# Seven half-width block products in place of eight in the output projection of an attention and SwiGLU kernel

## The chip, the cores and the metric

The kernel runs on one core of one Trainium2 chip. The metric is device time in microseconds (us) of one execution. Most executions agree within 0.3%. Three kinds of figures appear. Total times and ratios come from timed rounds. Stage lengths come from a profiled execution. The span in a profile is 1.6 to 2.1 us shorter than the time of the same execution.

## The reference

Sliding-window attention (batch 8, 8 heads, 576 positions, head size 64, window 32 to each side), then a SwiGLU block on the 4608 tokens: 512 features in, 1536 hidden, 512 out.

```python
attn = softmax(where(|i - j| <= 32, q @ k.T / 8, -1e9))
x    = (attn @ v) as [4608, 512]
out  = (silu(x @ w_gate) * (x @ w_val)) @ w_out
```

## The kernel before

The tokens are worked off in nine chunks of 512, counted from 0. In each chunk twelve units produce the gate and value products (TensorE), silu (ScalarE) and their product `hT` (VectorE). Then a stage follows that multiplies `hT` by `w_out`. This stage is interleaved with the attention of the next chunk: four tiles m to m+3, each with scores (`s_mm`), exponential on ScalarE (`s_exp`), mask on VectorE (`s_mask`), value matmuls (`a_mm`), normalization on VectorE (`a_norm`), and a transposing DMA into the next chunk's `xT` (`x_dma`). In the timelines below each engine starts its instructions in the order of the program. Matmuls add up their results in tiles of the accumulation memory PSUM; I call such a tile of 128 x 512 fp32 numbers a bank. I call "the stage" the time from its first score matmul to the first gate matmul of the next chunk. The code is shortened, with short lines joined.

```python
htpool = ...tile_pool(name="ht", bufs=2)
ps_a = ...tile_pool(name="ps_a", bufs=3, PSUM)   # scores, values, u_ps
ps_o = ...tile_pool(name="ps_o", bufs=2, PSUM)   # gate products, output products
# ... cut ...
def ffn2_part(j, sub, lo, hi):
    if lo == 0:
        obs[sub] = ps_o.tile([128, 512], FP32, tag="o", name="ob")
    for fk in range(lo, hi):
        nc.tensor.matmul(out=obs[sub], lhsT=hts[j][:, fk, 128*sub:128*sub+128],
                         rhs=wo16[:, fk, :], start=(fk == 0), stop=(fk == FKS - 1))
# ... cut ...
def ffn2(j, m):
    s_group((m, m + 1)); s_mask(m); s_mask(m + 1)
    ffn2_part(j, 0, 0, 6); ffn2_part(j, 0, 6, FKS)
    s_group((m + 2, m + 3))
    a_group((m,)); x_dma(m)
    s_mask(m + 2); s_mask(m + 3)
    ffn2_part(j, 1, 0, 8); ffn2_out(j, 0)
    a_group((m + 1, m + 2, m + 3))
    for i in (1, 2, 3): x_dma(m + i)
    ffn2_part(j, 1, 8, FKS); ffn2_out(j, 1)
    for sub in (2, 3):
        ffn2_part(j, sub, 0, FKS); ffn2_out(j, sub)
# ... cut ...
for j in range(1, NCH):
    a = ffn1_two(j)                      # units 0 and 1
    for u in range(2, FKS):
        ffn1_unit(j, u)
        if u == 2 and j + 1 < B: fetch(j + 1, a)      # GpSimd issues v and token loads
        if u >= 8 and j + 1 < B: shift(j + 1, 2 * (u - 8) + 1)   # two v copies on VectorE
    if j + 1 < NCH: ffn2(j, 4 * j + 4)
```

Of the kernel before, what the change touches and what calls it, by code (L numbers as in the profile page):

```python
# [7 lines left out]
FP32 = mybir.dt.float32  # L8
FP16 = mybir.dt.float16
# [3 lines left out]
ALU = mybir.AluOpType  # L13
# [3 lines left out]
def general_path(tc, keep, ident, weights, q, k, v, out):  # L17
# [6 lines left out]
    FKS = wg16.shape[2] // 128  # L24
    GS = d_model // 128
    BIG = 1.0e9
    with ExitStack() as st:
# [78 lines left out]
        with tc.For_i(0, B * S, 128) as r:  # L106
            xn = sb.tile([128, d_model], FP32, name="g_xn")
            nc.sync.dma_start(out=xn, in_=xd[bass.ds(r, 128), :])
            xT = sb.tile([128, GS, 128], FP16, name="g_xT")
            for g in range(GS):  # L110
                px = ps.tile([128, 128], FP32, name="g_px")
# [3 lines left out]
            for f in range(FKS):  # L115
                gv = ps.tile([128, 2, 128], FP32, name="g_gv")
                for i, w in enumerate((wg16, wv16)):
                    for g in range(GS):
                        nc.tensor.matmul(out=gv[:, i, :], lhsT=w[:, g, 128 * f:128 * f + 128],
                                         rhs=xT[:, g, :], start=(g == 0), stop=(g == GS - 1))  # L120
                sl = sb.tile([128, 128], FP16, name="g_sl")
# [12 lines left out]
def kernel(  # L134
# [10 lines left out]
    nc = tc.nc  # L145

    B, H, S, D = q.shape
    d_model, d_ff = moe_w_gate.shape
# [5 lines left out]
    NCH = n_tokens // 512  # L154
    FKS = d_ff // 128
    GS = d_model // 128
    SLABS = (0, 2, 4, 6, 9, 12)
    LONG = 2
    TP = 9
# [5 lines left out]
    fast = ctx.enter_context(ExitStack())  # L165
    const = fast.enter_context(tc.tile_pool(name="const", bufs=1))
# [5 lines left out]
    xtpool = fast.enter_context(tc.tile_pool(name="xt", bufs=3))  # L172
    htpool = fast.enter_context(tc.tile_pool(name="ht", bufs=2))
    spool = fast.enter_context(tc.tile_pool(name="sp", bufs=4))
    opool = fast.enter_context(tc.tile_pool(name="op", bufs=4))
    ps_a = fast.enter_context(tc.tile_pool(name="ps_a", bufs=3, space=bass.MemoryType.PSUM))
    ps_o = fast.enter_context(tc.tile_pool(name="ps_o", bufs=2, space=bass.MemoryType.PSUM))
    fast.enter_context(tc.manual_schedule())

    ident = keep.tile([128, 128], FP16)  # L180
    wg16 = keep.tile([128, GS, d_ff], FP16)
    wv16 = keep.tile([128, GS, d_ff], FP16)
    wo16 = keep.tile([128, FKS, d_model], FP16)
# [11 lines left out]
    kT = [const.tile([128, HP, S + 64], FP16, name=f"kT{i}") for i in range(2)]  # L195
    qT = [const.tile([128, HP, S], FP16, name=f"qT{i}") for i in range(2)]
    v16 = [const.tile([128, NT, H, 66], FP16, name=f"v16{i}") for i in range(2)]

    def after(dma, inst):
        tc.add_manual_dep(  # L200
            dma.ins, inst.ins.name,
            mybir.DependencyInfo(mybir.DependencyClass.Sync, mybir.DependencyReason.DATA),
            reason="load order")

    def cp_act(o, i):
        return nc.scalar.activation(out=o, in_=i, func=AF.Copy, bias=0.0, scale=1.0)  # L206

    def cp_dve(o, i):
        nc.vector.tensor_copy(out=o, in_=i)  # L209
# [13 lines left out]
    def load_long16(src, b, x):  # L223
        return long_dma((nc.gpsimd, nc.gpsimd), st16.tile([128, 2, TP * D], FP16, tag="st16", name="st16"),
                        src, b, x)
# [36 lines left out]
    def load_v(b, blocks, gate=None):  # L262
        vb = v[b].rearrange("h s d -> s h d")
        for m in blocks:
            lo, hi = max(0, 128 * m - 32), min(S, 128 * m + 96)
            p0 = lo - (128 * m - 32)
            d = nc.gpsimd.dma_start(out=v16[b % 2][p0:p0 + hi - lo, 2 * m, :, 0:D], in_=vb[lo:hi])  # L267
            if gate is not None:
                after(d, gate)

    def shift_v(b, t0, t1, lo, hi):
        vb = v16[b % 2]
        if lo:
            lo(vb[0:64, t0:t1:2], vb[64:128, t0 - 1:t1 - 1:2])
        if hi:
            hi(vb[64:128, t0:t1:2], vb[0:64, t0 + 1:t1 + 1:2])

    def load_w(s, which):
        c0, c1 = 128 * SLABS[s], 128 * SLABS[s + 1]
        for i in which:  # L280
            w, w16 = ((moe_w_gate, wg16), (moe_w_val, wv16))[i]
            nc.gpsimd.dma_start(
                out=w16[:, :, c0:c1],
                in_=w.rearrange("(g p) c -> p g c", p=128)[:, :, c0:c1])
# [6 lines left out]
    def load_tok(src, b, gate=None):  # L291
        st = stpool.tile([128, 5, H, D], FP16, tag="st", name="tok")
        sb = src[b].rearrange("h s d -> s h d")
        for m in range(5):
            n = min(128, S - 128 * m)
            d = nc.gpsimd.dma_start(out=st[0:n, m], in_=sb[128 * m:128 * m + n])  # L296
            if gate is not None:
                after(d, gate)
        return st
# [58 lines left out]
    def s_mask(m):  # L358
        p = pts[m].rearrange("p g i h q -> p (g i h q)")
        nc.vector.tensor_tensor(out=p, in0=p, in1=mask.rearrange("p a q -> p (a q)"),  # L360
                                op=ALU.mult)
# [32 lines left out]
    def x_out(m):  # L394
        j, i4 = divmod(m, 4)
        if j not in xts:
            xts[j] = xtpool.tile([128, 4, GS, 128], FP16, tag="xt", name="xT")
        return xts[j][:, i4]
# [15 lines left out]
    def x_dma(m):  # L414
        x16 = x16s.pop(m).rearrange("p a h d -> p (a h d)")
        nc.sync.dma_start_transpose(out=x_out(m), in_=x16)

    hts = {}
# [40 lines left out]
    def ffn1_two(j):  # L459
        for lo in (0, 256):  # L460
            for fk in range(2):
                ffn1_mm(j, fk, lo, 256, lo)
        return [ffn1_out(j, fk, 0, 512) for fk in range(2)][0]
# [13 lines left out]
    def ffn2_out(j, sub, parts=1):  # L477
# [5 lines left out]
            nc.sync.dma_start(out=out[r0:r0 + 128, c:c + w], in_=osb[:, c:c + w])  # L483
        return a

    def ffn2_last(j, sub):
        r0 = 512 * j + 128 * sub
        for c, w in ((0, 256), (256, 128), (384, 128)):
            ob = ps_o.tile([128, 512], FP32, tag="o", name="ob")
            for fk in range(FKS):  # L490
                nc.tensor.matmul(  # L491
                    out=ob[:, 0:w],
                    lhsT=hts[j][:, fk, 128 * sub:128 * sub + 128],
                    rhs=wo16[:, fk, c:c + w],
                    start=(fk == 0), stop=(fk == FKS - 1))
            osb = opool.tile([128, d_model], FP32, tag="osb", name="osb")
            cp_dve(osb[:, 0:w], ob[:, 0:w])
            nc.scalar.dma_start(out=out[r0:r0 + 128, c:c + w], in_=osb[:, 0:w])
# [60 lines left out]
    kq = []  # L559
    for s in range(len(SLABS) - 1):  # L560
        if s == 2:
            shift_v(0, 5, 6, cp_pool, cp_pool)
            shift_v(0, 7, 8, cp_pool, cp_pool)
        if s == len(SLABS) - 2:
            kq.append((load_long16(k, 1, 0), kT[1], 0, 32))
# [57 lines left out]
    for u in range(2):  # L623
        ffn1_unit(0, u, 256, 256)
    nc.vector.tensor_copy(
        out=mask, in_=band.unsqueeze(1).to_broadcast([128, 4 * HP, 64]))
# [20 lines left out]
    def fetch(b, gate):  # L647
        if len(toks[b]) == 1:
            toks[b].append(load_tok(q, b, gate))
        load_v(b, range(5), gate)  # L650
        if b + 1 < B:
            toks[b + 1] = [load_tok(k, b + 1), load_tok(q, b + 1)]
        kt, qt = toks.pop(b)
        turn_tok(kt, kT[b % 2], 32)
        turn_tok(qt, qT[b % 2], 0)

    def s_group(ms):
        for m in ms:
            s_mm(m)
            s_exp(m)  # L660

    def a_group(ms):
        for m in ms:
            a_mm(m)
            a_norm(m)
# [31 lines left out]
    def ffn2(j, m):  # L697
        s_group((m, m + 1))
        s_mask(m)
        s_mask(m + 1)  # L700
        ffn2_part(j, 0, 0, 6)
        ffn2_part(j, 0, 6, FKS)
        s_group((m + 2, m + 3))
        a_group((m,))
        x_dma(m)
        s_mask(m + 2)
        s_mask(m + 3)
        ffn2_part(j, 1, 0, 8)
        ffn2_out(j, 0)
        a_group((m + 1, m + 2, m + 3))  # L710
        for i in (1, 2, 3):
            x_dma(m + i)
        ffn2_part(j, 1, 8, FKS)
        ffn2_out(j, 1, 2 if j == NCH - 2 else 1)
        for sub in (2, 3):
            ffn2_part(j, sub, 0, 6)
            ffn2_part(j, sub, 6, FKS)
            ffn2_out(j, sub, 2 if j == NCH - 2 and sub in (2, 3) else 1)

    ffn2_first(4)  # L720
    for j in range(1, NCH):
        a = ffn1_two(j)
        for u in range(2, FKS):
            ffn1_unit(j, u)
            if u == 2 and j + 1 < B:
                fetch(j + 1, a)
            if u >= 8 and j + 1 < B:
                shift(j + 1, 2 * (u - 8) + 1)
        if j + 1 < NCH:
            ffn2(j, 4 * j + 4)  # L730
        else:
            good = check_range()
            for sub in range(3):
                ffn2_part(j, sub, 0, 6)
                ffn2_part(j, sub, 6, FKS)
                if sub == 1:
                    count_good(good)
                ffn2_out(j, sub, 2)
            ffn2_last(j, 3)
# [35 lines left out]
```

## Time and profile before

| | before |
|---|---|
| median time, 3 runs | 329.0 us |
| TensorE, VectorE, ScalarE busy | 98%, 49%, 46% |
| chain that ended last, TensorE's part | 94% |
| stage of each of the chunks 1 to 7 | 13.0 us |

In a timeline row the first number is the start in us from the span's begin, the second the length. `x12` means twelve instructions merged. A bracket gives the idle time of that engine before the row and what ended it; idle times up to 0.15 us get no bracket. The pages and rows of the kernel before stand in the prediction.

### The profile page before, as it was taken

To read this page: it belongs to the slowest core of one execution; us is meant where nothing else is said; L and a number is where in the kernel's file an instruction comes from. 1 tells how busy PE (TensorE), PEld (TensorE's weight loads), DVE (VectorE), ACT (ScalarE), POOL (GpSimd) and SP (SyncE) were. 2 spreads that over 40 slices of the span, in tenths; PEclk is the share of its full clock that TensorE was granted. 3 is DMA by queue.
4 is the path that set the end of the run, shared out by engine and by line. 5 is a ranking of instruction groups with operands and counts; after the bars stand their busy time and mean duration, and the time that the engine had idled before them with its cause. 6 is when DMAs were issued, how large, how long until landed. Compare 5 with 4: busy or idle time off the path is not lost.

```text
span 326.8 us, 6917 instructions
## 1 busy us (share of the span) xinstructions
PE 319.5 (98%) x2769; PEld 169.6 (52%) x2769; DVE 160.1 (49%) x319; ACT 151.3 (46%) x215; POOL 104.6 (32%) x136
## 2 busy tenths in 40 slices
PE   7999999999999999999999999999999999999994
PEld 5564546445554555455644564456445644564443
DVE  5754874457145734474347524762367143714421
ACT  4843675337443724372536453544355434643320
POOL 8964605964096007800680048203100000000000
PEclk9999999999999999999999999999999999999999
DMA  9999999999999959994999489988913400150012
GB/s 154 184 199 203 199 143 191 137 156 154 204 132 149 83 134 165 151 109 104 182 138 135 99 146 131 155 112 166 149 19 64 131 0 2 50 146 2 1 54 82
DMA packets 155190, 40.14 MB, mean 123 GB/s; under 512 B 140816, under 2 KB 151184, under 8 KB 155152
## 3 DMA queue, kind: packets, MB, share of 16 engines
q0 software_dynamic: 102640, 18.59, 76.5%
q1 hardware_dynamic: 51936, 20.49, 32.8%
q10 hardware_dynamic: 576, 0.56, 0.6%
q8 instruction: 23, 0.38, 0.5%
q14 instruction: 15, 0.12, 0.1%
HBM read 37.75 MB, written 9.44 MB: 144 GB/s over the span
## 4 chain that ended last, share of the span: by engine, by line
PE 94%; POOL 3%; DMA 2%; issue 0%; DVE 0%; POOLq 0%; DVEq 0%
PE g_ps L424 29%; PE u_ps L424 29%; PE ob L471 29%; PE o_ps L377 3%; PE s_ps L343 3%; DMA wg<-in_moe_w_gate_dram 2%; POOL v L267 1%; POOL st L213 1%; PE ob L491 1%; PE t_ps L248 1%; PE xt_ps L404 0%; DVE osb L209 0%; POOL iota L525 0%; PE cnt L515 0%; DVEq L209 0%
## 5 line engine op out<-in xcount | busy, mean ns | idle before, releaser
L451 DVE TENSOR_TENSOR hT<-ssb,u_ps 128x512 f16<-128x512 f16 (+1 forms) x110 | 74.5, 678 | 130.2 <-PE u_ps L424 78.1
L424 PE MATMUL g_ps<-xT,wg 128*128 128x512 f16 (+1 forms) x504 | 114.0, 349 | 0.2 <-DMA wg<-in_moe_w_gate_dram 0.2
L424 PE MATMUL u_ps<-xT,wv 128*128 128x512 f16 (+1 forms) x504 | 114.0, 349 | 0.0
L449 ACT ACTIVATE ssb<-g_ps 128x512 f16<-128x512 f32 (+1 forms) x110 | 64.7, 589 | 100.9 <-PE g_ps L424 100.5
L471 PE MATMUL ob<-wo,hT 128*128 128x512 f16 x420 | 95.5, 380 | 0.0
L424 PEld LDWEIGHTS <-wv 128*128 128x128 f16 x504 | 49.3, 98 | 44.2
L424 PEld LDWEIGHTS <-wg 128*128 128x128 f16 x504 | 48.9, 98 | 43.4 <-DMA wg<-in_moe_w_gate_dram 0.3
L267 POOL DMA_DIRECT2D v<-in_v_dram x40 | 33.7, 863 | 91.1 <-ACT ssb L449 90.0
L471 PEld LDWEIGHTS <-hT 128*128 128x128 f16 x420 | 39.0, 98 | 44.3
L206 ACT ACTIVATE osb<-ob 128x512 f32<-128x512 f32 x35 | 21.0, 599 | 51.9 <-PE ob L471 51.9
L353 ACT ACTIVATE p_t<-s_ps 128x1024 f16<-128x1024 f32 x36 | 34.9, 1022 | 4.7 <-PE s_ps L343 4.6
L296 POOL DMA_DIRECT2D tok<-in_k_dram x30 | 25.3, 879 | 14.2 <-ACT osb L206 12.6
L296 POOL DMA_DIRECT2D tok<-in_q_dram x30 | 25.5, 854 | 11.7 <-DMA v<-in_v_dram 4.8
L360 DVE TENSOR_TENSOR p_t<-p_t,mask 128x1024 f16<-128x1024 f16 x32 | 21.4, 688 | 9.3 <-ACT p_t L353 9.2
L389 DVE TENSOR_TENSOR x<-o_ps,rall 128x512 f16<-128x512 f32 x36 | 24.9, 691 | 1.2
L209 DVE COPY v<-v 64x528 f16<-64x528 f16 x60 | 18.5, 308 | 2.3 <-DMA v<-in_v_dram 0.4
L343 PEld LDWEIGHTS <-kT 64*128 64x128 f16 x576 | 9.7, 95 | 8.1 <-issue 7.2
L377 PEld LDWEIGHTS <-p_t 128*64 128x64 f16 x576 | 10.9, 110 | 4.9 <-DVE p_t L360 3.0
L377 PE MATMUL o_ps<-v,p_t 128*64 128x66 f16 x576 | 13.1, 196 | 0.2 <-ACT p_t L353 0.2
L343 PE MATMUL s_ps<-qT,kT 64*128 64x64 f16 x576 | 12.1, 191 | 0.1
L449 ACT ACT_TABLE_LOAD x8 | 10.3, 1283 | 0.1
L353 ACT ACT_TABLE_LOAD x8 | 10.3, 1283 | 0.1
(59 smaller groups left out, 87.6 us busy)
## 6 DMA issues: line engine op xcount, KB each, us to landing
out_dram<-osb SPq DMA_DIRECT2D x29, 256.0 KB, 2.3
v<-in_v_dram POOLq DMA_DIRECT2D x24, 128.0 KB, 6.4
tok<-in_k_dram POOLq DMA_DIRECT2D x24, 128.0 KB, 8.7
tok<-in_q_dram POOLq DMA_DIRECT2D x24, 128.0 KB, 9.8
v<-in_v_dram POOLq DMA_DIRECT2D x16, 96.0 KB, 6.3
wo<-in_moe_w_out_dram POOLq DMA_DIRECT2D x3, 512.0 KB, 9.2
out_dram<-osb SPq DMA_DIRECT2D x12, 128.0 KB, 1.8
st<-in_q_dram POOLq DMA_DIRECT2D x8, 144.0 KB, 6.5
```

The costliest lines, as they stand in the source:

```text
L206: return nc.scalar.activation(out=o, in_=i, func=AF.Copy, bias=0.0, scale=1.0)
L267: d = nc.gpsimd.dma_start(out=v16[b % 2][p0:p0 + hi - lo, 2 * m, :, 0:D], in_=vb[lo:hi])
L296: d = nc.gpsimd.dma_start(out=st[0:n, m], in_=sb[128 * m:128 * m + n])
L343: nc.tensor.matmul(out=sts[m][:, g, i, hp, :], lhsT=kT[b % 2][64 * g:64 * g + 64, hp, 64 * t:64 * t + 128], rhs=qT[b % 2][64 * g:64 * g + ...
L353: nc.scalar.activation(out=p.rearrange("p g i h q -> p (g i h q)"), in_=s.rearrange("p g i h q -> p (g i h q)"), func=AF.Exp, bias=0.0, sc ...
L360: nc.vector.tensor_tensor(out=p, in0=p, in1=mask.rearrange("p a q -> p (a q)"), op=ALU.mult)
L377: nc.tensor.matmul(out=o[64 * i:64 * i + 64, h // 4, 66 * (h % 4):66 * (h % 4) + 66], lhsT=p[:, g, i, hp, :], rhs=v16[b % 2][:, t, h, :], ...
L389: nc.vector.tensor_tensor(out=x16, in0=ov[:, :, :, 0:D], in1=r.unsqueeze(3).to_broadcast([128, 2, 4, D]), op=ALU.mult)
L424: nc.tensor.matmul(out=ps[:, at:at + n], lhsT=w[:, g, 128 * fk:128 * fk + 128], rhs=xts[j][:, lo // 128:(lo + n) // 128, g, :], start=(g = ...
L449: a = nc.scalar.activation(out=ssb[:, 0:n], in_=ps[0][:, 0:n], func=AF.Silu, bias=0.0, scale=1.0)
L451: nc.vector.tensor_tensor(out=hts[j][:, fk, lo:lo + n], in0=ssb[:, 0:n], in1=ps[1][:, 0:n], op=ALU.mult)
L471: nc.tensor.matmul(out=obs[sub], lhsT=hts[j][:, fk, 128 * sub:128 * sub + 128], rhs=wo16[:, fk, :], start=(fk == 0), stop=(fk == FKS - 1))
```

## The change

A 2x2x2 split of the product (tokens, hidden, output columns each in two halves) is computed with seven block products of a Strassen type and not eight. The aim is to take an eighth of TensorE's work out of this product in chunks 1 to 7. It is paid for with sums of fp16 blocks on VectorE (`sum_a` on `hT` each chunk, `sum_b` on `w_out` once), three fp32 snapshots of partial sums on ScalarE and three output additions on VectorE. A snapshot is a copy of a partial sum out of its bank, taken before the bank takes in the next product. The core of the diff, shortened and with lines joined:

```diff
+    def sum_a(j, i, lo, hi):       # s1 = a21+a22, s2 = s1-a11, s3 = a11-a21, s4 = a12-s2
+        ...
+    def prod(ps, lhs, rhs, first):
+        for kk in range(KH):                      # KH = 6
+            for i in range(2):
+                nc.tensor.matmul(out=ps[:, 256*i:256*i+256], lhsT=lhs[:, kk, 128*i:128*i+128],
+                                 rhs=rhs[:, kk], start=(first and kk == 0 and i == 0), ...)
+    def ffn2_seven(j, m):
+        s_group((m, m + 1)); s_mask(m); s_mask(m + 1)
+        sum_a(j, 3, KH - 2, KH)
+        x = bank(); prod(x, a11, b11, True); p1 = keep_act(x)
+        z = bank(); prod(z, s1, t1, True)
+        s_group((m + 2, m + 3)); a_group((m,)); x_dma(m)
+        s_mask(m + 2); s_mask(m + 3)
+        prod(x, s2, t2, False); u2 = keep_act(x)
+        a_group((m + 1, m + 2, m + 3)); x_dma(m + 1) ... x_dma(m + 3)
+        prod(x, s3, t3, False); u3 = keep_act(x)
+        y = ps_a.tile(...); prod(y, a12, b21, True)
+        put_sum(j, z, u3, 1, 1); put_sum(j, y, p1, 0, 0)
+        prod(x, a22, t4, False); o = out_tile(); cp_act(o, x); put(j, o, 1, 0)
+        prod(z, s4, b22, False); put_sum(j, z, u2, 0, 1)
     ...
             ffn1_unit(j, u)
+            if j == 1 and 2 <= u < 6: sum_b(u - 2)
+            if j + 1 < NCH:
+                if u in (4, 6):     sum_a(j, 2, ...)           # 768 elements
+                if u in (7, 9, 11): sum_a(j, 0, ...); sum_a(j, 1, ...)   # 512 each
+                if u == 10:         sum_a(j, 3, 0, KH - 2)     # 1024
             if u >= 8 and j + 1 < B: shift(j + 1, 2 * (u - 8) + 1)
-            ffn2(j, 4 * j + 4)
+            ffn2_seven(j, 4 * j + 4)
```

More of the change, by code (lines that the diff above doesn't have):

```diff
@@ L156 @@
     GS = d_model // 128
+    KH = FKS // 2
+    CH = d_model // 2
     SLABS = (0, 2, 4, 6, 9, 12)
@@ L174 @@
     spool = fast.enter_context(tc.tile_pool(name="sp", bufs=4))
+    snap = fast.enter_context(tc.tile_pool(name="sn", bufs=3))
     opool = fast.enter_context(tc.tile_pool(name="op", bufs=4))
@@ L197 @@
     v16 = [const.tile([128, NT, H, 66], FP16, name=f"v16{i}") for i in range(2)]
+    sumA = [const.tile([128, KH, 256], FP16, name=f"sa{i}") for i in range(4)]
+    sumB = [const.tile([128, KH, CH], FP16, name=f"sb{i}") for i in range(4)]
     def after(dma, inst):
@@ L484, in ffn2_out, with comb, sum_b @@
         return a
+    def comb(o, a, b, op):
+        nc.vector.tensor_tensor(out=o, in0=a, in1=b, op=op)
+    def sum_b(i):
+        b11, b12 = wo16[:, 0:KH, 0:CH], wo16[:, 0:KH, CH:]
+        b21, b22 = wo16[:, KH:, 0:CH], wo16[:, KH:, CH:]
+        t1, t2, t3, t4 = sumB
+        o, a, b = ((t1, b12, b11), (t2, b22, t1), (t3, b22, b12), (t4, b21, t2))[i]
+        comb(o, a, b, ALU.subtract)
+    def sum_a(j, i, lo, hi):
+        h = hts[j]
+        a11, a12 = h[:, lo:hi, 0:256], h[:, KH + lo:KH + hi, 0:256]
+        a21, a22 = h[:, lo:hi, 256:512], h[:, KH + lo:KH + hi, 256:512]
+        s1, s2, s3, s4 = [t[:, lo:hi] for t in sumA]
+        o, a, b, op = ((s1, a21, a22, ALU.add), (s2, s1, a11, ALU.subtract),
+                       (s3, a11, a21, ALU.subtract), (s4, a12, s2, ALU.subtract))[i]
+        comb(o, a, b, op)
@@ new lines, in prod, with bank, keep_act @@
+    def prod(ps, lhs, rhs, first):
+        for kk in range(KH):
+            for i in range(2):
+                nc.tensor.matmul(out=ps[:, CH * i:CH * i + CH],
+                                 lhsT=lhs[:, kk, 128 * i:128 * i + 128], rhs=rhs[:, kk],
+                                 start=(first and kk == 0 and i == 0),
+                                 stop=(kk == KH - 1 and i == 1), skip_group_check=True)
+    def bank():
+        return ps_o.tile([128, 512], FP32, tag="o", name="ob")
+    def keep_act(ps):
+        t = snap.tile([128, 512], FP32, tag="sn", name="sn")
+        cp_act(t, ps)
+        return t
@@ new lines, in out_tile, with put, put_sum @@
+    def out_tile():
+        return opool.tile([128, d_model], FP32, tag="osb", name="osb")
+    def put(j, o, row, col):
+        r0 = 512 * j + 256 * row
+        nc.sync.dma_start(
+            out=out[r0:r0 + 256, CH * col:CH * col + CH].rearrange("(i p) c -> p i c", p=128),
+            in_=o.rearrange("p (i c) -> p i c", i=2))
+    def put_sum(j, ps, sn, row, col):
+        o = out_tile()
+        comb(o, ps, sn, ALU.add)
+        put(j, o, row, col)
+    def ffn2_seven(j, m):
+        h = hts[j]
+        a11, a12, a22 = h[:, 0:KH, 0:256], h[:, KH:, 0:256], h[:, KH:, 256:512]
+        b11, b21, b22 = wo16[:, 0:KH, 0:CH], wo16[:, KH:, 0:CH], wo16[:, KH:, CH:]
+        s1, s2, s3, s4 = sumA
+        t1, t2, t3, t4 = sumB
+        s_group((m, m + 1))
+        s_mask(m)
+        s_mask(m + 1)
+        sum_a(j, 3, KH - 2, KH)
+        x = bank()
+        prod(x, a11, b11, True)
+        p1 = keep_act(x)
+        z = bank()
+        prod(z, s1, t1, True)
+        s_group((m + 2, m + 3))
+        a_group((m,))
+        x_dma(m)
+        s_mask(m + 2)
+        s_mask(m + 3)
+        prod(x, s2, t2, False)
+        u2 = keep_act(x)
+        a_group((m + 1, m + 2, m + 3))
+        for i in (1, 2, 3):
+            x_dma(m + i)
+        prod(x, s3, t3, False)
+        u3 = keep_act(x)
+        y = ps_a.tile([128, 512], FP32, tag="a", name="y_ps")
+        prod(y, a12, b21, True)
+        put_sum(j, z, u3, 1, 1)
+        put_sum(j, y, p1, 0, 0)
+        prod(x, a22, t4, False)
+        o = out_tile()
+        cp_act(o, x)
+        put(j, o, 1, 0)
+        prod(z, s4, b22, False)
+        put_sum(j, z, u2, 0, 1)
@@ L726 @@
                 fetch(j + 1, a)
+            if j == 1 and 2 <= u < 6:
+                sum_b(u - 2)
+            if j + 1 < NCH:
+                if u in (4, 6):
+                    sum_a(j, 2, 3 * (u - 4) // 2, 3 * (u - 4) // 2 + 3)
+                if u in (7, 9, 11):
+                    sum_a(j, 0, u - 7, u - 5)
+                    sum_a(j, 1, u - 7, u - 5)
+                if u == 10:
+                    sum_a(j, 3, 0, KH - 2)
             if u >= 8 and j + 1 < B:
```

## The prediction

> **What bounds the kernel now.** I read the page first: busy shares, then the chain that ended last.
>
> ```profile
> PE 319.5 (98%) x2769; PEld 169.6 (52%) x2769; DVE 160.1 (49%) x319; ACT 151.3 (46%) x215; POOL 104.6 (32%) x136
> ...
> PE g_ps L424 29%; PE u_ps L424 29%; PE ob L471 29%; PE o_ps L377 3%; PE s_ps L343 3%; DMA wg<-in_moe_w_gate_dram 2%; POOL v L267 1%; POOL st L213 1%; PE ob L491 1%; PE t_ps L248 1%; PE xt_ps L404 0%; DVE osb L209 0%; POOL iota L525 0%; PE cnt L515 0%; DVEq L209 0%
> ```
>
> TensorE is on the chain for 94% of the span, and the output product (ob, L471) is 29% of it. Only this third can shrink. Second, the timeline of one chunk (the fourth) from the end of its gate and value products: TensorE, then ScalarE, then VectorE. Columns: start, length (us), engine, line, operation, count, and the idle time before with its releaser.
>
> ```profile
> 141.93 0.64 PE L343 MATMUL s_ps<-qT,kT 64*128 64x64 f16 x32
> 142.50 2.76 PE L471 MATMUL ob<-wo,hT 128*128 128x512 f16 x12
> 145.20 0.64 PE L343 MATMUL s_ps<-qT,kT 64*128 64x64 f16 x32
> 145.77 0.45 PE L377 MATMUL o_ps<-v,p_t 128*64 128x66 f16 x16
> 146.15 1.90 PE L471 MATMUL ob<-wo,hT 128*128 128x512 f16 x8
> 147.98 0.97 PE L377 MATMUL o_ps<-v,p_t 128*64 128x66 f16 x48
> 148.88 6.22 PE L471 MATMUL ob<-wo,hT 128*128 128x512 f16 x28
> 154.93 0.60 PE L424 MATMUL g_ps<-xT,wg 128*128 128x256 f16 x4
> 155.37 0.60 PE L424 MATMUL u_ps<-xT,wv 128*128 128x256 f16 x4
> ```
> ```profile
> 141.78 1.28 ACT L353 ACT_TABLE_LOAD   x1
> 143.08 1.94 ACT L353 ACTIVATE p_t<-s_ps 128x1024 f16<-128x1024 f32 x2
> 145.65 1.94 ACT L353 ACTIVATE p_t<-s_ps 128x1024 f16<-128x1024 f32 x2 [0.63 <-PE s_ps L343]
> 147.47 0.60 ACT L206 ACTIVATE osb<-ob 128x512 f32<-128x512 f32 x1
> ```
> ```profile
> 141.09 0.62 DVE L209 COPY v<-v 64x528 f16<-64x528 f16 x2
> 142.10 0.69 DVE L451 TENSOR_TENSOR hT<-ssb,u_ps 128x512 f16<-128x512 f16 x1 [0.39 <-PE u_ps L424]
> 142.82 0.62 DVE L209 COPY v<-v 64x528 f16<-64x528 f16 x2
> 144.13 0.69 DVE L360 TENSOR_TENSOR p_t<-p_t,mask 128x1024 f16<-128x1024 f16 x1 [0.69 <-ACT p_t L353]
> 145.05 0.69 DVE L360 TENSOR_TENSOR p_t<-p_t,mask 128x1024 f16<-128x1024 f16 x1 [0.22 <-ACT p_t L353]
> 146.26 0.21 DVE L388 RECIPROCAL rall<-o_ps 128x8 f32<-128x8 f32 x1 [0.52 <-PE o_ps L377]
> 146.50 0.69 DVE L389 TENSOR_TENSOR x<-o_ps,rall 128x512 f16<-128x512 f32 x1
> 147.11 1.28 DVE L360 TENSOR_TENSOR p_t<-p_t,mask 128x1024 f16<-128x1024 f16 x2
> ```
>
> No TensorE row carries an idle bracket: the 13.00 us from 141.93 to 154.93 are all issue. But two things are tight. The attention for the next chunk runs inside this stage, and its last two masks end at 147.11 + 1.28 = 148.39, while the last of the 48 value matmuls' three tiles starts about 147.98 + 2 x 0.30 = 148.58. Slack: 0.2 us. Any gain on TensorE ahead of that point must be matched by ScalarE and VectorE.
>
> **What the Trainium skill says.** "TensorE: Matmul & The Clock Gate", section Back-to-back issue gap, gives an isolated gap of N/2.4 + 2.5 ns: 109 ns for 256 columns and 216 for 512. The trace agrees: four 256-column matmuls, each with its own weight load, start 0.44 us apart as a group (154.93 to 155.37), 109 ns each; twenty-eight of 512 columns take 6.05, 216 each. (The same section's 131 ns for loaded pairs of 512 is not what this trace shows.) "VectorE: DVE Perf Modes", section The perf-mode tier table, has an elementwise operation on two 16-bit SBUF tensors at twice the rate of one with a PSUM input; the trace agrees (1024 fp16 masks and 512 products with PSUM both take 688 to 691 ns). Its errata section's (N+151)/0.96 ns gives 691 for 512 elements and 424 for 256; the trace has 690 and 416. "ScalarE: Activation LUTs", section What ACT_TABLE_LOAD costs, has 1283 ns plus a drain of 1380; the trace shows 1283, and the exponential 1.30 us after the load began, so only the first counts here.
>
> **The change part by part.**
> *TensorE.* Per chunk it removes 48 matmuls of 512 columns, 48 x 0.216 = 10.36 us, and adds 7 products x 6 x 2 = 84 of 256 columns, 84 x 0.109 = 9.17. Gain 1.19; one more switch from attention to products costs about 0.1 (12 matmuls after the scores took 2.70, not 2.59). Net 1.1 us, times seven chunks 7.7: the ceiling is 329.0 - 7.7 = 321.3, if nothing waits.
> *ScalarE.* Three snapshots and one output copy stand in for four copies: 4 x 0.60 both ways. But the first snapshot moves between the exponentials of the second and third tile.
> *VectorE.* Added sums are 2x fp16 operations; from the rate of the mask, 512 elements 0.42, 768 0.55, 1024 0.69 us. Per chunk 6 x 0.42 + 2 x 0.55 + 0.69 + 0.42 = 4.7, and three output additions reading PSUM, 3 x 0.69 = 2.1: 6.8 us x 7, plus four weight sums of 1536 (0.95 each) once: 51 us. VectorE goes to about 211 us, two thirds busy; the mean is harmless, its place is not.
> *DMA.* Same output bytes, in rows of half the length; output lands in 2.3 us and nothing waits for it.
>
> **Where it waits.** I set time 0 at the first score matmul (141.93) and step through VectorE's new order from unit 9 of the chunk, whose product is ready 2 x 1.73 us before that of unit 11 (0.17), at -3.28. Start-to-start: product then dependent sum or copy 0.72; sum to dependent sum 0.45; sum to copy 0.44; copy pair 0.62; product to independent sum, and mask to mask, 0.60 (all from neighbouring rows).
> Unit 9: 0.72 + 0.45 + 0.44 + 0.62, free at -1.05. Unit 10 is ready at -1.55 so it is late: product 0.61, 1024-sum 0.71, copies 0.62, free at 0.89. Unit 11: 0.72, 0.45, 0.44, 0.62, free at 3.12, though the exponential it awaits was done at 2.2. Masks of tiles 0 and 1 start at 3.12 and 3.72, the rest of the last sum at 4.32, reciprocal and normalization of tile 0 at 4.66 and 4.90, masks of tiles 2 and 3 at 5.51 and 6.11, ending 6.20 and 6.80.
> ScalarE: exponentials end at 3.09, snapshot to 3.69, exponentials of tiles 2 and 3 end at 4.72 and 5.69: before VectorE reaches them.
> TensorE: scores 0.57, two products 2.72, scores 0.57: 3.86. Values of tile 0 need the mask (3.81 plus some 0.08): 3.89 to 4.27. Third product to 5.68, values of tile 1 to 5.98. Tile 2 waits for 6.28, tile 3 for 6.88, ending 7.18. Four products, 0.1 + 5.24: 12.52. Then the next chunk's second gate bank waits for the output addition: end of product +0.2 +0.69 +0.06 = 0.95 after, against 0.87: 0.08.
> So the stage takes 12.6 instead of 13.0: of 1.1 us some 0.7 goes back in waits. In chunk 7 there are no value copies; there the masks follow ScalarE (tile 3's exponential at 5.69, mask to 6.5), and the stage takes about 12.3. Sum of gains: 6 x 0.4 + 0.7 = 3.1 us: **325.9**.
>
> **Rivals.**
> *Full gain, 321.3 to 322:* only if ScalarE were out of the way. For it: 98% busy TensorE. Against: even with VectorE free at once, table load, four exponentials and the snapshot put the fourth mask's end at 6.5 where TensorE asks for it at about 6.3; that floor alone is 0.3 per chunk, so about 323.7 is the best I believe.
> *VectorE becomes the bound, sums at half the rate:* the strided halves of hT might not run at two elements per cycle. Then some 1.9 us more (0.27 per 512 elements, 3584 of them from unit 9 on) reach the masks and each stage is 1.5 over the old: about 338. Against: each inner run is 256 contiguous fp16.
> *Waits eat all:* if independent operations overlap less than I took, another 0.4 per chunk, 328.5.
> *Late transposes:* the x transposes start when the normalization of the last tile ends, about 9.4; three took 4.5 us of issue from their first, so the last lands near 13.5 and is needed at 12.6 + 1.75 = 14.3. Hidden, with less slack than before.
>
> **Range and chances.** Best case 323.7, everything eaten 328.5, so 323.6 to 328.6 holds it 8 times in 10. Faster by 2% means under 322.4, below my floor: 5%. Slower by 2% (335.6) only by the half-rate sums: 4%. Within 2%: 91%.
>
> **What would show it.** Right: TensorE groups of twelve 256-column matmuls lasting 1.31 us; sums at 0.42/0.55/0.69; VectorE without idle from unit 9 to the fourth mask; TensorE or its weight loads idle some 0.3 us each before the value tiles 2 and 3, with the mask (L366 of the changed kernel) named; no idle in the last four products. Wrong if: sums take 0.69 for 512 elements; 256-column matmuls alternating between two halves of a bank run slower than 109 ns; ScalarE snapshots hold the third or fourth product; or the next chunk's first products wait for transposes.

## The result, and the profile after

The changed kernel takes 327.59 us (median of 4, 327.19 to 328.02) against 329.01 (328.98 to 329.67) of the kernel before in the same rounds. The ratio is 0.9952, 95% interval 0.9933 to 0.9972. Ratios here are the mean time of one kernel's fast runs over that of the other's fast runs of the same rounds, so they are not quite the ratio of the medians. It is a little faster, and within 2%.

The page of the changed kernel, busy shares and the first line of the chain that ended last:

```profile
PE 314.9 (97%) x3021; PEld 195.2 (60%) x3021; DVE 208.5 (64%) x414; ACT 151.2 (46%) x215; POOL 104.6 (32%) x136
...
PE 56%; DMA 13%; issue 13%; DVE 9%; POOL 7%; ACT 0%; POOLq 0%; SPq 0%; DVEq 0%
```

VectorE's busy time rose from 160 to 208 us, and TensorE's part of the chain fell from 94% to 56%. VectorE's masks now stand in it (3%), but so do token loads (9%) and stretches of "issue" (13%), while TensorE was busy for 97% of the span. So the page says that something changed and not what; that is read from the stage. The timeline of the same stage as in the prediction (fourth chunk, number 3), TensorE:

```profile
142.19 0.64 PE L349 MATMUL s_ps<-qT,kT 64*128 64x64 f16 x32
142.76 1.48 PE L514 MATMUL ob<-wo,hT 128*128 128x256 f16 x12
144.08 1.47 PE L514 MATMUL ob<-sb,sa 128*128 128x256 f16 x12
145.49 0.64 PE L349 MATMUL s_ps<-qT,kT 64*128 64x64 f16 x32
146.17 0.45 PE L383 MATMUL o_ps<-v,p_t 128*64 128x66 f16 x16
146.55 1.48 PE L514 MATMUL ob<-sb,sa 128*128 128x256 f16 x12
147.97 1.03 PE L383 MATMUL o_ps<-v,p_t 128*64 128x66 f16 x32
149.15 0.45 PE L383 MATMUL o_ps<-v,p_t 128*64 128x66 f16 x16 [0.15 <-DVE p_t L366]
149.53 1.48 PE L514 MATMUL ob<-sb,sa 128*128 128x256 f16 x12
...
154.78 0.60 PE L430 MATMUL g_ps<-xT,wg 128*128 128x256 f16 x4
```

A product of twelve takes 1.32 us start to start (142.76 to 144.08) and 1.31 at the end of the stage (152.16 to 153.47), 109 to 110 ns per matmul; 109 was expected. But the 48 value matmuls of tiles 1 to 3 occupy 147.97 to 149.53, 1.56 us, where they took 0.90 before: they wait for masks. A bracket shows only 0.15 of that, because the end of a matmul in the profile lies after the moment at which the next may start. So read starts, not brackets. The weight loads show more of it: 0.25 and 0.27 us idle before tiles 2 and 3, ended by the mask (L366), close to the 0.3 that the prediction named as its sign. VectorE in that stage:

```profile
143.86 0.42 DVE L493 TENSOR_TENSOR sa<-hT 128x512 f16<-128x512 f16 x1
144.32 0.42 DVE L493 TENSOR_TENSOR sa<-sa,hT 128x512 f16<-128x512 f16 x1
144.78 0.62 DVE L215 COPY v<-v 64x528 f16<-64x528 f16 x2
145.42 1.29 DVE L366 TENSOR_TENSOR p_t<-p_t,mask 128x1024 f16<-128x1024 f16 x2
146.63 0.42 DVE L493 TENSOR_TENSOR sa<-hT,sa 128x512 f16<-128x512 f16 x1
...
147.81 1.28 DVE L366 TENSOR_TENSOR p_t<-p_t,mask 128x1024 f16<-128x1024 f16 x2
```

The first mask starts 3.23 us after the stage (2.20 before) and directly behind the value copies, with no bracket: it waits for VectorE's own queue and no longer for the exponential.

Stage lengths per chunk (differences of two starts in the timeline of one profiled execution, us), with those of the experiments. The totals come from different rounds, so compare kernels by the ratio:

| chunk | 1 | 2 to 6 | 7 | total us (fast median) | ratio to before |
|---|---|---|---|---|---|
| before | 13.0 | 13.0 | 13.0 | 329.0 | |
| after | 13.52 | 12.60 | 12.18 | 327.59 | 0.9952 |
| e1, stale sums (wrong result) | 13.60 | 12.2 | 12.18 | 325.03 | 0.9871 |
| e2, no first snapshot (wrong result) | 13.24 | 12.61 | 12.18 | 327.24 (one run) | |
| e3, copies shared with ScalarE | 12.64 | 12.2 | 12.18 | 324.66 | 0.9865 |
| e4, other order on TensorE | 12.95 | 12.46 | 12.33 | 328.81 | 0.9998 |
| e5, copies deferred | 12.77 | 12.2 | 12.18 | 325.15 | 0.9865 |
| e6, both of these | 12.42 | 12.2 | 12.18 | 324.99 | 0.9865 |
| e7, no masks (wrong result) | 13.62 | 11.8 | 11.80 | 322.74 | 0.9787 |
| e8, two sums doubled | 13.89 | 13.51 | 12.18 | 333.92 (one run) | |
| e9, late token issue | 12.62 | 12.60, chunk 2 12.84 | 12.17 | 327.32 | 0.9945 |
| e10, e6 and e9 together | 12.18 | 12.2, chunk 2 12.66 | 12.18 | 324.51 | 0.9868 |

Beside the stages, the next chunk's gate and value products became 0.06 to 0.07 us longer in the changed kernel (20.92 or 20.93 against 20.86), because the second gate bank is held by the last output addition: in the fourth chunk that ends at 155.67 and the bank's first matmul starts at 155.72, 0.50 us after the group before it, where these groups are otherwise 0.44 apart. The last chunk starts at 288.61 in the profile after, 290.34 before: 1.73 us earlier. The profiled spans, 326.2 and 326.8, differ by less. The profiled execution of before was the shortest of its kind: the spans of 25 later executions are 326.9 to 328.7, so I draw nothing from the difference after the last chunk.

The exception is chunk 1. VectorE in the changed kernel there:

```profile
74.78 1.02 DVE L215 COPY v<-v 64x528 f16<-64x528 f16 x2
75.84 0.69 DVE L457 TENSOR_TENSOR hT<-ssb,u_ps 128x512 f16<-128x512 f16 x1
...
77.47 0.87 DVE L215 COPY v<-v 64x528 f16<-64x528 f16 x2
```

The pairs of copies take 1.02 and 0.87 us in place of 0.62, and one copy before them (unit 8) waited 0.24 us for its transfer. The masks of chunk 1 begin at 78.38, 4.16 us after the stage's start at 74.22, and tile 0 stalls TensorE for 0.9 us.

### The profile page after: what moved, and what is told of

Its sections match the earlier page's. It is cut to its first block, busy times and chain, and to the rows that moved or that the text cites. A ratio compares the mean times of both kernels' runs of the same rounds, so it can differ in the third digit from the quotient of the medians.

```text
span 326.2 us, 7522 instructions
## 1 busy us (share of the span) xinstructions
PE 314.9 (97%) x3021; PEld 195.2 (60%) x3021; DVE 208.5 (64%) x414; ACT 151.2 (46%) x215; POOL 104.6 (32%) x136
## 4 chain that ended last, share of the span: by engine, by line
PE 56%; DMA 13%; issue 13%; DVE 9%; POOL 7%; ACT 0%; POOLq 0%; SPq 0%; DVEq 0%
PE g_ps L430 19%; PE u_ps L430 19%; PE ob L514 7%; DMA tok<-in_k_dram 6%; PE ob L477 6%; POOL v L273 4%; DVE p_t L366 3%; DMA tok<-in_q_dram 3%; POOL tok L302 3%; PE y_ps L514 2%; DMA wg<-in_moe_w_gate_dram 2%; DVE v L215 1%; DMA kT<-tok 1%; PE o_ps L383 1%; DVE sa L493 1%
## 5 line engine op out<-in xcount | busy, mean ns | idle before, releaser
L514 PEld LDWEIGHTS <-sa 128*128 128x128 f16 x336 | 31.6, 98 | 4.3 <-DVE sa L493 0.2
L514 PE MATMUL ob<-sb,sa 128*128 128x256 f16 x252 | 31.2, 273 | 0.0
L302 POOL DMA_DIRECT2D tok<-in_k_dram x30 | 25.3, 872 | 13.6 <-ACT osb L212 12.3
L514 PEld LDWEIGHTS <-hT 128*128 128x128 f16 x252 | 24.1, 98 | 3.1
L366 DVE TENSOR_TENSOR p_t<-p_t,mask 128x1024 f16<-128x1024 f16 x32 | 20.9, 686 | 3.0 <-ACT p_t L359 2.8
L215 DVE COPY v<-v 64x528 f16<-64x528 f16 x60 | 20.1, 335 | 2.0 <-DMA v<-in_v_dram 0.2
L212 ACT ACTIVATE sn<-ob 128x512 f32<-128x512 f32 x21 | 12.6, 599 | 18.5 <-PE ob L514 18.4
L212 ACT ACTIVATE osb<-ob 128x512 f32<-128x512 f32 x14 | 8.4, 597 | 25.1 <-PE ob L514 14.2
L477 PE MATMUL ob<-wo,hT 128*128 128x512 f16 x84 | 19.4, 379 | 0.0
L383 PE MATMUL o_ps<-v,p_t 128*64 128x66 f16 x576 | 15.5, 197 | 3.3 <-DVE p_t L366 2.0
L493 DVE TENSOR_TENSOR osb<-ob,sn 128x512 f32<-128x512 f32 x14 | 9.7, 692 | 13.9 <-PE ob L514 13.5
L493 DVE TENSOR_TENSOR sa<-hT 128x512 f16<-128x512 f16 (+1 forms) x35 | 16.6, 475 | 0.7
```

The source lines that it names most:

```text
L215: nc.vector.tensor_copy(out=o, in_=i)
L302: d = nc.gpsimd.dma_start(out=st[0:n, m], in_=sb[128 * m:128 * m + n])
L366: nc.vector.tensor_tensor(out=p, in0=p, in1=mask.rearrange("p a q -> p (a q)"), op=ALU.mult)
L477: nc.tensor.matmul(out=obs[sub], lhsT=hts[j][:, fk, 128 * sub:128 * sub + 128], rhs=wo16[:, fk, :], start=(fk == 0), stop=(fk == FKS - 1))
L493: nc.vector.tensor_tensor(out=o, in0=a, in1=b, op=op)
L514: nc.tensor.matmul(out=ps[:, CH * i:CH * i + CH], lhsT=lhs[:, kk, 128 * i:128 * i + 128], rhs=rhs[:, kk], start=(first and kk == 0 and i = ...
```

## The experiments

Theory V: TensorE's gain is real, and it is given back because the masks of the next chunk's tiles are queued on VectorE behind the new sums. Rival P: the half-width products cost more than counted. Rival S: the first snapshot on ScalarE delays the exponentials. Theory G, for chunk 1: GpSimd's issuing of transfers slows the copies.

**e1, the sums taken out of VectorE's queue.** From chunk 2 on the products read the sums of chunk 1. The result is wrong, the matmuls are the same.

```diff
-            if j + 1 < NCH:
+            if j == 1:
                 if u in (4, 6):
```
(and the same condition at the last `sum_a` in the stage)

> Wrong result on purpose: the block sums of hT are formed in chunk 1 only, later chunks multiply the stale sums. All matmuls, snapshots and output additions stay. Theory V (VectorE reaches the masks late because the sums lie ahead of them in its queue): the stage of chunks 2 to 6, from the first score matmul to the next chunk's first gate matmul, falls from 12.60 us to about 12.2, where the exponentials of tiles 2 and 3 gate the masks; chunk 1 keeps its 13.5; total about 325.6. Rival P (the 256-column products or the snapshots cost the time themselves): the stages stay at 12.6 and the total within 0.3 of 327.6.

Measured: 12.2 us in chunks 2 to 6, 325.03 us, ratio 0.9871 (0.9854 to 0.9887). VectorE's first masks in the fourth chunk:

```profile
144.04 0.69 DVE L366 TENSOR_TENSOR p_t<-p_t,mask 128x1024 f16<-128x1024 f16 x1 [0.70 <-ACT p_t L359]
144.95 0.69 DVE L366 TENSOR_TENSOR p_t<-p_t,mask 128x1024 f16<-128x1024 f16 x1 [0.22 <-ACT p_t L359]
```

The brackets are back: with the sums gone VectorE is idle and waits for exponentials, as in the kernel before. Theory V holds; rival P does not. The run takes both load and queue length off VectorE; e5 separates the two.

**e2, the first snapshot left out** (a blank tile is added in its place; wrong result).

```diff
-        p1 = keep_act(x)
+        p1 = blank
```

> Wrong result on purpose: the first snapshot, which sits on ScalarE between the exponentials of tiles 1 and 2, is dropped and a blank tile is added in its place. Theory V: exponential 2 cannot start before its scores (about 3.75 us into the stage) in either case and VectorE is later still, so the stage of chunks 2 to 6 stays at 12.6 (within 0.1). Rival S (the snapshot delays the exponentials by 0.6 and these hold the masks): the stage falls to about 12.0 to 12.1.

Measured: 12.61 us in chunks 2 to 6, as with the snapshot. Rival S falls: while VectorE is late, ScalarE is not what holds the masks. Chunk 1 came out at 13.24 in place of 13.52. Its first mask started 3.89 us into the stage in place of 4.16: two pairs of copies took 0.90 and 0.96 us, and none waited for a transfer.

**e3, one value copy of each pair to ScalarE**, in units 8 to 10. Correct.

```diff
-                shift(j + 1, 2 * (u - 8) + 1)
+                t = 2 * (u - 8) + 1
+                shift_v(j + 1, t, t + 1, cp_act if u < 11 else cp_dve, cp_dve)
```

> Correct result: in units 8 to 10 one of the two value copies goes from VectorE to ScalarE, which is idle 1.13 us per unit there; nothing else moves. VectorE is 3 x 0.31 = 0.93 us earlier at the masks. Theory V: stage of chunks 2 to 6 about 12.2, total about 325.3. Rival P or S: 12.6 and 327.6. Chunk 7 has no value copies and stays at 12.2.

Measured: 12.2 us, 324.66 us, ratio 0.9865 (0.9848 to 0.9881). Taking other work from the same queue does what taking the sums did.

**e4, half of the product a12 b21, and the product before it, moved ahead of the value matmuls of tiles 2 and 3.** Correct.

```diff
-        a_group((m + 1, m + 2, m + 3))
-        prod(x, s3, t3, False)
-        u3 = keep_act(x)
-        y = ps_a.tile(...)
-        prod(y, a12, b21, True)
+        a_group((m + 1,))
+        y = ps_a.tile(...)
+        prod(y, a12, b21, True, 0, KH // 2)
+        prod(x, s3, t3, False)
+        u3 = keep_act(x)
+        a_group((m + 2, m + 3))
+        prod(y, a12, b21, True, KH // 2, KH)
```
(`x_dma` follows each group; cut)

> Correct result: order of TensorE alone. Half of the product a12 b21 is put between the third product and the fourth, the fourth goes ahead of the value matmuls of tiles 2 and 3, which follow it with the other half. The masks get 2 us more. Theory V: waits at tiles 2 and 3 vanish, stage of chunks 2 to 7 about 12.0, chunk 1 still waits 0.9 at tile 0 (about 12.9), total about 323.5 to 324.5. Danger: the x transposes of tiles 2 and 3 start about 0.9 us later; if they are late, the next chunk's first products wait and the gain is about halved.

Measured: 12.46 us, not 12.0, and 328.81 us in total, ratio 0.9998. A miss. The waits at tiles 2 and 3 are gone (their 32 matmuls follow at once), but two others came. The last product starts at 153.15, 0.3 us after the one before it allows, since the output addition that frees its bank now queues behind the normalizations. And the next chunk's weight loads wait for the x transposes, twice in this execution. The wait list of the weight loads (us in total, times, longest):

```profile
PEld L430 <- DMA xT<-x: 1.9, 2, 1.0
```

The gate and value products of these two chunks took 0.8 and 0.9 us longer. The danger named in the expectation was real: in the changed kernel the sum of these waits is 0.3 us. The four executions fall into two pairs, 328.0 and 328.1 against 329.6 and 329.8 us; the profiled one is of the faster pair, and what the slower ones waited for is not shown.

**e5, value copies deferred behind the output additions**, where the stage at hand does not read them. Correct; the same instructions, in another order.

```diff
-                shift(j + 1, 2 * (u - 8) + 1)
+                t = 2 * (u - 8) + 1
+                if t <= 6 - j:
+                    shift(j + 1, t)
+                else:
+                    late.append(t)
     ...
         put_sum(j, y, p1, 0, 0)
+        shift_late(j, 2)
     ...
         put_sum(j, z, u2, 0, 1)
+        shift_late(j, 4)
```

> Correct result: the value copies that the stage at hand does not need (block 7 always; block 5 from chunk 2, block 3 from chunk 4, block 1 in chunk 6) are moved on VectorE behind the output additions. Same instructions, other order; nothing on ScalarE or TensorE changes. Theory V (what matters is the length of VectorE's queue ahead of the masks): stage of chunks 2 to 6 12.2 us as with the copies on ScalarE, chunk 1 about 12.65 (one pair, 0.87 there, leaves the queue), total about 324.7. If it is VectorE's total work that counts: 12.6 and 327.6.

Measured: 12.2 us, 325.15 us, ratio 0.9865 (0.984 to 0.989). VectorE does as much as in the changed kernel (busy 207.1 us against 208.5), so it is the place in the queue that counts and not the load.

**e6, deferral, and of the copies that stay one of each pair on ScalarE.** Correct.

```diff
                 if t <= 6 - j:
-                    shift(j + 1, t)
+                    shift_v(j + 1, t, t + 1, cp_act, cp_dve)
```

> Correct result: as the deferral, and of the copies that must stay ahead one of each pair goes to ScalarE. Theory V: chunks 2 to 6 stay at 12.2 (there the exponentials gate), chunk 1 falls to about 12.3, total about 324.3; the best correct version of the study.

Measured: 324.99 us, ratio 0.9865 (0.9845 to 0.9885), the same as e3 and e5; chunk 1 at 12.42. Not 324.3, and no better than the simpler e3.

**e7, the masks left out** (wrong result). This sizes the ceiling.

```diff
-        s_mask(m)
-        s_mask(m + 1)
-        s_mask(m + 2)
-        s_mask(m + 3)
```

> Wrong result on purpose: the four masks of each stage are left out, so the value matmuls wait for exponentials alone (done 5.7 us into the stage, before TensorE asks at 6.2). All sums, snapshots and products stay. Theory V with the ceiling as predicted: stage of chunks 2 to 7 11.9 us, which is 13.0 less the net 1.1 of TensorE; total about 322. If the products themselves had waits of their own (snapshots, additions, alternating halves of a bank), the stage would stay above 12.1.

Measured: 11.8 us in chunks 2 to 7, 322.74 us, ratio 0.9787 (0.9761 to 0.9814, so it stays open whether this is more than 2%). Two rows of TensorE: the first gate matmuls after chunk 1's stage, and the value matmuls of tiles 1 to 3 in the fourth chunk, which now follow each other in one row, 48 in 0.89 us from their start to the next product's:

```profile
88.12 0.60 PE L430 MATMUL g_ps<-xT,wg 128*128 128x256 f16 x4 [1.62 <-DMA xT<-x]
```
```profile
147.37 0.96 PE L383 MATMUL o_ps<-v,p_t 128*64 128x66 f16 x48
```

The gain of the products is 13.0 - 11.8 = 1.2 us a stage: all that was counted, without the 0.1 I had taken off for one more switch between kinds of matmul. Chunk 1 shows the next wall: its products end in time, then TensorE stands 1.6 us for the x transposes.

**e8, the two sums of unit 11 done twice.** Correct.

```diff
+                if u == 11:
+                    sum_a(j, 0, u - 7, u - 5)
+                    sum_a(j, 1, u - 7, u - 5)
```

> Correct result: the two sums of unit 11 are done twice, 0.9 us more VectorE work ahead of the masks and nothing else. Theory V: stage of chunks 2 to 6 from 12.60 to about 13.4 to 13.5; chunk 7, which has VectorE slack, from 12.18 to about 12.4 to 12.6; total about 331.5. Rival P: no change.

Measured: chunks 2 to 6 at 13.51 us, 0.91 more for 0.9 us of added sums: one for one. Chunk 7 stayed at 12.18; without value copies its slack took all of it, which I had not expected. One run, 333.92 us, where about 331.5 was expected: the stages account for 4.9 us over the changed kernel, and 1.4 us more are not explained.

**e9, the query tokens of batch 3 issued after chunk 1's stage.** Correct; VectorE's program is untouched.

```diff
-            toks[b + 1] = [load_tok(k, b + 1), load_tok(q, b + 1)]
+            toks[b + 1] = [load_tok(k, b + 1)]
+            if b != 2:
+                toks[b + 1].append(load_tok(q, b + 1))
     ...
-        cp_act(o, x)
+        mark = cp_act(o, x)
+        if j == 1:
+            toks[3].append(load_tok(q, 3, mark))
```

> Correct result: the changed kernel, but the query tokens of batch 3, whose transfers GpSimd issues through chunk 1's stage, are issued at that stage's end; VectorE's program is unchanged. Theory G (in chunk 1 the value copies take 1.02 and 0.87 us a pair, not 0.62, because GpSimd is issuing transfers at that moment): both pairs take about 0.62 and the stage of chunk 1 falls from 13.5 to about 12.9 (0.65 off). Rival (they are slow for another reason, or the late value transfer alone holds the queue): pairs still near 0.9 and the stage at 13.3 or more. Chunks 2 to 7 unchanged at 12.6 and 12.18; total about 327.0.

Measured: chunk 1's stage 12.62 us, and 327.32 us in total, ratio 0.9945 (0.993 to 0.996). The two pairs of copies that had been slow:

```profile
74.95 0.62 DVE L215 COPY v<-v 64x528 f16<-64x528 f16 x2
...
77.23 0.62 DVE L215 COPY v<-v 64x528 f16<-64x528 f16 x2
```

Theory G holds for the pairs. The edit takes away the transfers as well as their issuing, but the traces decide between the two. The DMA engines moved 153 GB/s during the first pair here and 155 during the slow one of the changed kernel. And of the 684 copies of this form in all twelve traces, the 518 that overlap no issuing instruction of GpSimd took 0.30 us at most. All 66 that took over 0.33 us began 0.23 to 0.74 us into such an instruction and ended 0.09 to 0.13 us after its end.

The stage fell by 0.9, not the 0.65 of the pairs alone, because the value transfer came in time too. Part of the gain was only moved: chunk 2 went from 12.60 to 12.84, and one pair there took 0.84. In total the intervals of e9 and of the changed kernel overlap, so a gain in time is not shown.

**e10, e6 and e9 together.** Correct (both edits as above).

> Correct result: deferral, ScalarE copies and the late query tokens together. Theory V with G: chunk 1 at about 12.2 like chunks 2 to 7, unless its x transposes arrive late; total about 324.5, about the same as the deferral with ScalarE copies (0.2 better at most).

Measured: chunk 1 at 12.18, 324.51 us, ratio 0.9868 (0.9848 to 0.9888), one slow run left out. As expected no better than e6; the correct versions e3, e5, e6 and e10 all beat both kernels, by 1.3% against before, where the changed kernel has 0.5%, and e3 is the least edit.

## Why the prediction was right or wrong

It was right: 327.59 lies in 323.6 to 328.6, and within 2% was the call. Its centre, 325.9, was 1.7 us too low, and one term explains most of that.

- *TensorE's rate and the ceiling.* 109 ns for 256 columns, also when two halves of a bank alternate: right. The ceiling was 1.1 us a stage, e7 shows 1.2. The formula (N+151)/0.96 that the prediction takes from the errata section stands there for fp32 additions; here it came within 2% for fp16 operations at half the count (0.42 us for 512 elements, where it gives 0.424).
- *Sizes of the sums.* 0.42, 0.55 and 0.69 us predicted; 0.42, 0.55 and 0.68 in the trace after. The rival of half-rate sums did not happen.
- *Where it waits, chunks 2 to 6.* The walk through VectorE's queue gave 12.52 us and 0.08 more in the next chunk; measured 12.60 and 0.06 to 0.07. The walk runs 0.1 us early from the first mask on (3.12 forecast, 3.23 in the trace). The cause was then tested from four sides: work out of the queue (e1, e3), work moved back in it (e5), work added (e8), the wait itself removed (e7).
- *Chunk 7.* Predicted about 12.3, measured 12.18. The masks of tiles 0 and 1 do follow ScalarE there. Those of tiles 2 and 3 do not: tile 3's exponential ends at 5.69 us, its mask starts at 5.81 behind VectorE's own work. That it ends at 6.49, forecast 6.5, is luck; the last point of this list says what held it.
- *The step that was mis-sized:* the term "6 x 0.4" of the sum treated chunks 1 to 6 alike. Chunk 1 is not like the others. Its copies take 1.02 and 0.87 us a pair while GpSimd issues transfers, and one waits for data, so its stage took 13.52 us where the sum has 12.6: 0.9 us lost. The kernel before had a slow pair there too (0.80 us) and two waits of 0.20 for transfers, with VectorE idle around them, and its stage did not feel it. I took the copy time from the fourth chunk alone. How the loss splits between slow copies and late transfers differs between executions: e1, which runs the same program up to there, lost as much (13.60) with one slow pair (1.01) and waits of 0.65 and 0.37 for transfers.
- *The rest of the difference.* From the profiles the last chunk starts 1.73 us earlier, where the sum has 3.1: of that gap of 1.4, chunk 1 takes 0.9, the second gate bank 0.06 in each of six later chunks where I had put it inside the 12.6 (with the stage at 12.60 on its own), and one wait for transposes in chunk 7 about 0.15; chunk 7's stage gave 0.1 back. The 0.3 left between 1.4 and 1.7 lies outside these stretches and is not explained.
- *Late transposes.* Predicted hidden with less slack. Nearly right: 0.3 us on the weight loads in one chunk. e4 and e7 show how near that wall is.
- *"Even with VectorE free at once" about 0.3 per chunk stays.* e1, e3 and e5 all stop at 12.2, 0.4 above the e7 stage. The exponential of tile 3 ends 5.69 us into the stage in all of them, where I had put it, but it is not what holds the last mask, as the prediction and the expectations of e1 and e6 have it. VectorE in e5, fourth chunk (stage from 141.20):

```profile
145.56 0.21 DVE L394 RECIPROCAL rall<-o_ps 128x8 f32<-128x8 f32 x1 [0.21 <-PE o_ps L383]
145.81 0.69 DVE L395 TENSOR_TENSOR x<-o_ps,rall 128x512 f16<-128x512 f32 x1
146.41 1.28 DVE L366 TENSOR_TENSOR p_t<-p_t,mask 128x1024 f16<-128x1024 f16 x2
```

The exponentials of tiles 2 and 3 ended at 145.97 and 146.89; the masks start at 146.41 and 147.01, directly behind the normalization of tile 0, which itself waits for TensorE's value matmuls. So VectorE's order holds them, and the exponential would be the next limit about 0.1 us earlier (an estimate: 5.69 + 0.03 against 5.81). Tile 3's value matmuls start 6.55 us into the stage here and 6.20 in e7: that is nearly all of the 0.4. Masks ahead of the normalization were not run.

So of the 1.2 us that seven products save in each stage, chunks 2 to 6 give 0.8 back to the masks (11.8 to 12.6), and e5 got 0.4 of it back by order alone.

## What to carry to other kernels

When the busiest engine's work is cut, look for the point in its program where another engine's result is due, and measure the slack there; here it was 0.2 us, so saving more than that ahead of the point was worth nothing without moving the other engines too. New work on a half idle engine costs what stands behind it in that engine's queue, and the cure can be order: the copies that no one needed yet were the cheapest thing to move. A duration taken from one chunk should be checked in the chunk with the most other traffic.

## What the Trainium skill lacked or had wrong

- "TensorE: Matmul & The Clock Gate", Back-to-back issue gap: it has 131 ns as the sustained spacing of loaded 512-column matmuls; this trace shows 216 (twenty-eight in 6.05 us), which is the section's figure for the isolated gap. For 256 columns that formula's 109 ns held with a weight load before every matmul, and with alternating halves of one bank, which the section does not mention.
- "ScalarE: Activation LUTs", What ACT_TABLE_LOAD costs: 1283 ns is what the trace has; of the drain of 1380 ns nothing is seen: the load starts 0.02 us after the end of the silu before it, and the exponential 1.30 us after the load's start.
- "VectorE: DVE Perf Modes", The DRAIN you can't avoid: the section says that a next operation that is not held starts earlier, and has no figure for how much. Here independent elementwise operations of 0.69 us start 0.60 to 0.61 us apart; dependent ones start 0.03 to 0.04 us after the end of the one before.
- "SBUF — State Buffer", Who interferes with whom, says that a copy in a two-port mode and GpSimd block each other for whole instructions. The runs agree in direction: a pair of fp16 copies took 0.62 us alone and 0.87 to 1.02 while GpSimd issued transfers, and 0.62 again when these were moved (e9). They do not agree on whole instructions: 52 copies that lay wholly inside an issuing instruction, and began in its first 0.24 us, took 0.29 us as if alone. For a copy held by an issue the page has no figure; here such a copy ended 0.09 to 0.13 us after the issue, 0.33 to 0.72 us long in place of 0.29.
